# A gated mix of segmented attention and a spectral filter on one core: keys put into order by the copies, wider score and value matmuls, and a new written-out order

## The chip, the cores and the metric

The kernel runs on one core of a Trainium2 chip. The metric is the device time of one execution in microseconds (us). The kernel before was timed in three runs. One more execution was profiled, and every duration here is from that one. Engines are named as the profile names them: PE (TensorE matmul), PEld (TensorE weight load, which overlaps PE), DVE (VectorE), ACT (ScalarE), POOL (GpSimd) and SP (SyncE, which issues most of the transfers).

## The reference

Two branches work on the same 2048 x 640 input, and a gate mixes them row by row. Branch A is attention with 32 heads of 20 over four segments of 512 tokens, each with a linear memory of the segments before it. Branch B multiplies a two-dimensional spectrum with learned weights.

```python
# A: per segment s of 4, 32 heads of 20
logits = einsum('bhqd,bhkd->bhqk', qs, ks) * scale + mask        # causal within 512 tokens
p = softmax(logits);  a_dot = einsum('bhqk,bhkd->bhqd', p, vs)
pq = where(qs > 0, qs + 1, exp(qs))
a_mem = einsum('bhld,bhde->bhle', pq, M) / (einsum('bhld,bhd->bhl', pq, z)[..., None] + 1e-6)
o = g * a_mem + (1 - g) * a_dot                                  # g = sigmoid(beta), per head
pk = phi(ks);  M += einsum('bhld,bhle->bhde', pk, vs);  z += pk.sum(l)
a = concat(o) @ wo
# B
X = rfft2(x) * (w_r + 1j * w_i);  b = irfft2(X).astype(bfloat16)
# mix, per row
g = sigmoid((x * gate_w).sum(-1));  out = g * a + (1 - g) * b
```

## The kernel before, in words

The program is first recorded as a list of operations (`Sched.op`), each with the engines that it may run on, its inputs and outputs and a cost. The tuple `ORDER` then names, for each place in the program, an operation (number // 2) and which of its engines runs it (number % 2). `schedule` does not choose any order: it walks `ORDER`, gives each operation its PSUM bank and its DMA semaphore by a small cost model, and `emit` writes the five in-order engine programs with the waits between them. In that model a matmul costs its columns (`PECOL`), a change of the PE's tile mode costs `COST`, and a transfer costs its time on 16 rings (`ring`). The model of before holds nothing of how an engine's program gets to the engine.

A TensorE operation is recorded by `mms`: a list of matmuls, each of them two instructions in the program, a weight load and a matmul (PE and PEld have 4796 and 4807 rows on the page). All have the line of the helper, L526 (L524 where the helper cuts a 128-wide weight in four). Copies out of PSUM have L535 on ACT and L537 on DVE.

The parts that the change touches:

- **Projection of keys and queries.** `proj_direct` (segment 0, four heads at a time in 32-column tiles) and `proj_tile` (segments 1 to 3, 128 columns). Queries stream all 512 tokens in one matmul. Keys are wanted in the token order 0-127, 256-383, 192-255 and 128-191, 448-511 and 384-447 (`KPOS` and the turned halves), and `token_order` gets it by streaming 2 x 256 tokens, two matmuls for every weight. The copy out of PSUM (`copy_alts`, 512 columns) then keeps the order.
- **Values.** `v_part` makes a block of 128 tokens; for every odd block the halves of 64 tokens are swapped, with four weight tiles of 32 columns for each of the five chunks.
- **Scores.** `qk_unit` does 80 units, each on all four banks of the pool "qk": kind 0 (12 matmuls), kind 1 (16 matmuls, two halves of 64 keys by 320 and 192 queries, four heads each) and kind 2 (24 small ones). The exponential (L1309, on ACT) follows each, the masks on POOL (L1330) follow that.
- **Probabilities times values.** `pv_flipped` (segments 0 to 2) runs `VPIECES`: six pieces by four heads, the last two being the halves of one block of 128 queries.

The start of the program sets much of the order around this. Segment 0's projections (`proj_direct`, names `xT,wq` and `xT,wk` with 32-column tiles) are the first real work of the PE, while the SP queue brings in weights, the input for branch B (`xsb`), tables and filter weights, one transfer after the other and with at most 1.6 MB under way. Segment 1's transposed input (`xT`, a transposing transfer, L558) comes behind them. From then on attention, branch B and the memory are interleaved in all engines until the output projection (L524 and `oTl`), which ends the program.

Of the kernel before, what the change touches and what calls it, by code (L numbers as in the profile page):

```python
# [12 lines left out]
P = 128  # L13
S = 2048
D = 640
H = 32
DH = 20
# [27 lines left out]
class Op:  # L45
    __slots__ = ("id", "alts", "preds", "succs", "prio", "banks", "nbytes", "npred", "eng", "t0", "t1",
                 "stamp", "need_inc", "dyn", "first", "outside", "name", "dma", "key", "xfer", "lock", "mode", "emode", "hold", "width")


class Sched:  # L50
    HOP = 70.0
    TIE = 0.15
    WINDOW = 1600000
# [7 lines left out]
    def op(self, alts, r=(), w=(), prio=0.0, nbytes=0, name="", after=(), dma=False, xfer=0.0, lock=False, mode=0, hold=False, width=16):  # L61
# [6 lines left out]
        o.xfer, o.lock, o.mode, o.hold, o.width = xfer, lock, mode, hold, width  # L68
# [36 lines left out]
        if name in ("gate_tab", "den_gate") and not o.banks:  # L105
# [5 lines left out]
            (0, 3): 105.0, (1, 3): 105.0, (2, 3): 105.0, (3, 0): 105.0, (3, 1): 105.0, (3, 2): 105.0}  # L111

    def schedule(self, pools, order, nsem=56):
# [14 lines left out]
        for i, o in enumerate(pe):  # L128
            o.emode = o.mode
            if o.mode < 0:  # L130
                modes = [held[id(b)] for b in o.banks if id(b) in held]
                if not modes and i and pe[i - 1].emode not in (1, 3):
                    modes = [pe[i - 1].emode]
                for q in pe[i + 1:] if not modes else ():
                    m = q.mode if q.mode >= 0 else held.get(id(q.banks[0]), -1)
                    if m >= 0:
                        modes = [0 if m in (1, 3) else m]
                        break
                o.emode = (modes + [0])[0]
            if o.emode not in (1, 3):  # L140
                for b in o.banks:
                    held[id(b)] = o.emode
# [3 lines left out]
        tied = [False]  # L146
        level = {k: {q: 0.0 for q in v} for k, v in pools.items()}
# [55 lines left out]
        while len(self.order) < len(order):  # L203
# [8 lines left out]
            o = queue[e][pos[e]]  # L212
            if e == "dve" and tied[0] and pos["pool"] < len(queue["pool"]):
                q = queue["pool"][pos["pool"]]
                if all(p.t1 is not None and p.t1 + self.HOP <= t + 30.0 for p in q.preds) and free["pool"] <= t + 1.0:
                    t += self.TIE * q.alts["pool"][1]
# [11 lines left out]
            free[e] = o.t1 = t + occ  # L228
            if e == "dve" and o.lock:
                port = t + occ  # L230
            if o.dma:
                if o.hold:
                    free[e] = max(free[e], max(ring) + 470.0)
# [236 lines left out]
VPIECES = ((0, 0, 512, 0), (1, 512, 384, 128), (2, 896, 192, 320), (2, 1088, 64, 256), (3, 1152, 64, 448), (3, 1216, 64, 384))  # L470
# [3 lines left out]
class Kern:  # L474
# [35 lines left out]
    def mms(self, items, r, w, prio, name="", extra=0.0, mode=0):  # L510
# [17 lines left out]
        op = self.Sc.op({"pe": (f, cost + 22.0 * (name == "qk"), 216.0 if name == "qk" else 141.0)}, r=r, w=w, prio=prio, name=name, mode=mode)  # L528
        return op
# [24 lines left out]
    def dma(self, dst, src, nbytes, r, w, prio, tr=False, name="", after=(), queue="sp"):  # L554
# [9 lines left out]
        if width == 16 and not tr and nbytes >= 200000 and name[:3] == "ld_":  # L564
# [7 lines left out]
        "ld_xn": (450.0, 950.0, 16), "ld_W": (670.0, 450.0, 16), "W_dup": (480.0, 900.0, 16), "ld_beta": (400.0, 120.0, 16), "ld_big": (500.0, 2900.0, 16), "ld_den": (520.0, 150.0, 16),  # L572
# [18 lines left out]
              ((1, 0, 0, 192, 0, 320), (1, 64, 64, 192, 0, 320), (2, 0, 0, 320, 320, 192), (2, 64, 64, 320, 320, 192)),  # L591
# [4 lines left out]
        0, 22, 28, 74, 72, 24, 2, 30, 4, 44, 6, 26, 8, 10, 36, 12, 42, 70, 14, 16, 34, 18, 176, 200, 20, 188, 32, 194, 182, 88, 178, 184, 196, 180,  # L596
        190, 187, 202, 192, 60, 206, 90, 208, 204, 199, 230, 93, 242, 48, 210, 218, 212, 220, 46, 232, 102, 222, 94, 50, 214, 76, 244, 216, 234, 97,
        224, 226, 62, 1070, 236, 78, 314, 238, 229, 81, 246, 1884, 248, 250, 241, 588, 83, 350, 253, 590, 352, 354, 98, 316, 84, 356, 338, 86, 266,
        116, 340, 268, 100, 358, 604, 105, 361, 318, 606, 270, 272, 320, 56, 274, 342, 106, 322, 52, 344, 118, 278, 40, 276, 280, 128, 628, 608, 324,
        54, 282, 130, 290, 630, 38, 346, 108, 292, 133, 326, 294, 328, 330, 110, 296, 112, 284, 349, 332, 632, 986, 298, 286, 300, 334, 135, 289,  # L600
        254, 992, 612, 336, 414, 592, 398, 58, 256, 136, 400, 114, 362, 139, 258, 614, 364, 402, 366, 368, 610, 370, 386, 994, 372, 260, 404, 388,
        622, 64, 390, 416, 980, 596, 140, 302, 624, 418, 1068, 598, 262, 392, 616, 304, 374, 120, 982, 306, 142, 376, 308, 420, 996, 310, 164, 264,
        378, 380, 618, 313, 382, 984, 394, 123, 384, 654, 397, 430, 1072, 600, 1886, 66, 432, 2050, 1888, 620, 988, 406, 434, 2052, 408, 2054, 594,
        2056, 68, 656, 1890, 410, 462, 634, 2058, 464, 1918, 166, 1892, 466, 436, 468, 1894, 412, 2060, 1920, 168, 1922, 124, 1924, 1896, 626, 470,
        1898, 472, 1926, 145, 516, 518, 1928, 520, 1900, 522, 127, 422, 1932, 524, 474, 424, 1902, 526, 1904, 1066, 476, 152, 1906, 478, 426, 480,
        1908, 482, 446, 154, 528, 484, 530, 448, 428, 532, 1910, 534, 157, 486, 438, 536, 450, 646, 1930, 538, 440, 542, 544, 648, 990, 546, 442,
        554, 548, 540, 556, 558, 550, 560, 488, 552, 500, 490, 502, 444, 492, 452, 562, 494, 650, 496, 564, 504, 506, 566, 498, 508, 652, 884, 568,
        2552, 510, 886, 454, 512, 704, 602, 456, 514, 2106, 888, 171, 2108, 458, 640, 158, 2110, 2112, 706, 643, 2114, 636, 2116, 1940, 1914, 1942,
        998, 2080, 460, 1944, 146, 2082, 639, 1912, 2084, 708, 686, 2086, 658, 644, 1952, 688, 2088, 1946, 1916, 2118, 2120, 2122, 2124, 160, 2126,
        1948, 1936, 570, 162, 1954, 1956, 173, 1951, 2128, 1934, 670, 2090, 2130, 878, 672, 1958, 2132, 1960, 880, 1938, 1974, 882, 872, 1963, 680,  # L610
        712, 1976, 660, 1964, 714, 1978, 1980, 1968, 914, 874, 682, 2134, 2136, 877, 2138, 674, 1982, 2140, 2142, 1985, 676, 2092, 1966, 916, 662,
        678, 919, 830, 2094, 664, 148, 832, 2144, 694, 834, 174, 2146, 1992, 2148, 838, 2096, 2098, 1970, 854, 696, 720, 666, 856, 1972, 2100, 2150,
        684, 722, 2152, 2154, 2160, 2172, 690, 2162, 2164, 2174, 1986, 2166, 836, 2168, 2176, 2178, 2170, 668, 1988, 2180, 2102, 2156, 728, 2104,
        2182, 842, 2184, 692, 2158, 730, 2038, 840, 844, 572, 2186, 2040, 846, 962, 1990, 860, 732, 744, 850, 964, 710, 698, 746, 967, 1998, 716,
        2042, 2000, 701, 862, 908, 734, 2044, 2046, 150, 2006, 1994, 2048, 762, 736, 865, 1996, 2008, 764, 920, 2066, 922, 932, 2010, 2189, 925, 718,
        2012, 910, 934, 2002, 738, 2014, 913, 752, 2191, 2004, 937, 724, 2016, 778, 2062, 848, 944, 755, 2018, 780, 748, 946, 2020, 949, 890, 892,
        766, 2022, 2024, 895, 726, 968, 2026, 974, 970, 2029, 976, 750, 972, 786, 740, 956, 979, 2030, 902, 788, 896, 898, 742, 958, 901, 950, 952,
        575, 2032, 790, 802, 961, 904, 782, 926, 955, 804, 756, 796, 907, 852, 866, 798, 759, 938, 868, 577, 928, 800, 940, 871, 760, 942, 770, 579,
        806, 931, 1008, 1010, 2078, 772, 1040, 2554, 2034, 1000, 2556, 1074, 1002, 2036, 2558, 1012, 2074, 1004, 2560, 1015, 2562, 702, 1042, 2064,
        1007, 774, 2288, 2565, 1044, 2586, 784, 2588, 2290, 1047, 1032, 2590, 1034, 2068, 1036, 1016, 2592, 776, 1039, 2070, 2594, 1018, 808, 2596,  # L620
        2280, 792, 1020, 858, 1048, 2282, 2600, 814, 794, 1050, 2076, 580, 768, 582, 1064, 2566, 1052, 2234, 816, 2072, 2284, 2346, 2236, 2568, 2238,
        2292, 2348, 2226, 2240, 1028, 2570, 1031, 2572, 2208, 2192, 2228, 2574, 2195, 2230, 810, 2232, 2576, 2320, 2210, 813, 2522, 2578, 2322, 2608,
        2212, 2524, 2214, 3220, 1116, 1118, 2610, 2526, 1120, 2612, 2528, 2530, 2244, 1123, 2262, 2294, 2580, 2246, 2296, 2264, 2248, 2266, 2614,
        2268, 1054, 2298, 2616, 2250, 2620, 2622, 2582, 2624, 2598, 1056, 2584, 1084, 1086, 1088, 2626, 1059, 2628, 1090, 2300, 2304, 2618, 2642,
        2631, 2324, 2306, 2216, 1076, 1078, 2218, 2632, 2270, 2302, 1080, 2220, 2644, 2272, 1082, 2222, 1142, 2338, 2314, 2602, 2274, 2252, 2276,
        2316, 1022, 2340, 1144, 2646, 2254, 2326, 2648, 2256, 2650, 2318, 2258, 1024, 1146, 1060, 2604, 2332, 2308, 1027, 2652, 2286, 2404, 1062,
        2335, 2654, 1092, 2310, 2406, 1108, 1110, 1148, 1094, 1112, 2312, 2774, 2776, 2778, 2780, 1115, 2656, 2342, 2782, 2328, 1096, 2350, 2828,
# [1028 lines left out]
```

## Time and profile before

| what | value |
|---|---|
| three runs | 254.83, 256.54, 258.51 us; median 256.54 |
| profiled execution | 252.51 us, of which the span from the first to the last instruction is 250.8 us |
| PE busy | 228.6 us (91%), 4796 matmul rows |
| PEld busy | 147.5 us (59%), 4807 rows |
| DVE, ACT, POOL busy | 199.3 us (79%), 197.4 us (79%), 159.8 us (64%) |
| mean granted TensorE clock | 0.992 |
| program transfers (queue q8, kind "instruction") | 38 packets, 0.62 MB |
| all transfers | 53532 packets, 41.00 MB, mean 163 GB/s |

A busy PE in this profile is not a PE at its peak: matmuls overlap, and the end of each is modelled. The profiled execution is 4.0 us below the median of the three runs.

### The profile page before, as it was taken

How to read it: one execution, taken by the hardware profiler on the slowest of the kernel's cores; microseconds unless marked ns; L12 is line 12 of the kernel's file. 1: busy time of each engine (PE TensorE's matmuls, PEld its weight loads, DVE VectorE, ACT ScalarE, POOL GpSimd, SP SyncE). 2: the span in 40 equal slices, each digit the busy share in tenths (PEclk: the TensorE clock that was granted, in tenths of full speed). 3: DMA queues.
4: the chain of work that ended last, by engine and by line, in shares of the span. 5: the costliest groups of instructions: out<-in, count | busy, mean ns of one | idle time of the engine just before them, and what ended most of it. 6: DMA issues, size and time to landing. Idle time of an engine off the chain costs nothing.

```text
span 250.8 us, 11077 instructions
## 1 busy us (share of the span) xinstructions
PE 228.6 (91%) x4796; PEld 147.5 (59%) x4807; DVE 199.3 (79%) x454; ACT 197.4 (79%) x232; POOL 159.8 (64%) x288
## 2 busy tenths in 40 slices
PE   7697699989989899998999997989999999999993
PEld 3465456666654476555656744545554667577782
DVE  1576387887999999979889996888989999983653
ACT  2265377899979999998989987989899998987320
POOL 8535572356977729396569936676479896689510
PEclk9999799999999999999999999999999999999999
DMA  7999902553354873579775778678168698856214
GB/s 224 287 275 296 269 14 64 118 112 77 86 143 137 208 184 101 145 194 205 202 180 169 203 198 233 178 157 226 64 209 205 168 268 119 128 97 132 95 62 107
DMA packets 53532, 41.00 MB, mean 163 GB/s; under 512 B 24684, under 2 KB 51308, under 8 KB 53484
## 3 DMA queue, kind: packets, MB, share of 16 engines
q1 hardware_dynamic: 52300, 39.62, 63.0%
q10 hardware_dynamic: 1184, 0.67, 1.1%
q8 instruction: 38, 0.62, 1.0%
q14 instruction: 10, 0.08, 0.1%
HBM read 21.94 MB, written 11.12 MB: 132 GB/s over the span
## 4 chain that ended last, share of the span: by engine, by line
PE 58%; DVE 17%; DMA 12%; ACT 6%; issue 3%; SPq 2%; POOL 0%; ACTq 0%; DVEq 0%
PE psum L526 53%; PE psum L524 5%; DMA Wt<-Wt 4%; ACT ex L1309 4%; DVE Ac L537 3%; DVE UV L1492 3%; DMA wk<-in_A_wk_dram 3%; DMA out_dram<-ot 3%; DMA gcc<-g_scr 2%; SPq L560 2%; DVE qu L537 1%; DVE ub L537 1%; DVE G L1534 1%; DVE Bt L537 1%; DVE mem L1203 1%
## 5 line engine op out<-in xcount | busy, mean ns | idle before, releaser
L1330 POOL TENSOR_SCALAR_AFFINE_SELECT ex<-ex 128x256 bf16<-128x256 bf16 (+2 forms) x224 | 121.5, 565 | 50.8 <-ACT ex L1309 48.1
L1309 ACT ACTIVATE ex<-psum 128x2048 bf16<-128x2048 f32 (+4 forms) x92 | 138.5, 1505 | 16.3 <-PE psum L526 14.4
L526 PE MATMUL psum<-xT,wk 128*32 128x256 bf16 (+1 forms) x470 | 38.0, 287 | 5.1 <-issue 3.6
L526 PE MATMUL psum<-xT,wq 128*32 128x512 bf16 (+1 forms) x224 | 33.4, 385 | 1.1 <-ACT xT L535 0.8
L526 PE MATMUL psum<-qkp 20*64 20x64 bf16 (+5 forms) x1280 | 32.4, 270 | 0.5 <-ACT ex L1309 0.2
L526 PE MATMUL psum<-wv,xT 128*32 128x320 bf16 (+3 forms) x400 | 31.3, 302 | 0.4 <-DVE va L1161 0.4
L526 PEld LDWEIGHTS psum<-xT,wk 128*32 128x32 bf16 (+1 forms) x470 | 22.6, 101 | 12.9 <-issue 7.3
L1492 DVE TENSOR_TENSOR UV<-psum,Wt 128x642 bf16<-128x642 f32 x32 | 25.0, 817 | 2.8 <-DMA Wt<-Wt 2.2
L526 PEld LDWEIGHTS psum<-qkp 20*64 20x64 bf16 x1280 | 13.3, 103 | 15.5 <-ACT ex L1309 9.1
L524 PE MATMUL psum<-wo,oU 128*32 128x320 bf16 x480 | 20.8, 300 | 0.0
L526 PEld LDWEIGHTS psum<-wv,xT 128*32 128x32 bf16 (+1 forms) x400 | 14.3, 96 | 9.1 <-issue 2.9
L526 PE MATMUL psum<-ex,va 128*32 128x64 bf16 (+3 forms) x576 | 17.4, 256 | 2.0 <-DVE Ac L537 0.8
L1161 DVE TENSOR_TENSOR va<-psum,ebx 128x320 bf16<-128x320 f32 x32 | 14.8, 479 | 5.4 <-PE psum L526 4.4
L526 PE MATMUL psum<-big,Ac 128*128 128x160 bf16 (+2 forms) x96 | 17.6, 258 | 0.8 <-DVE va L1161 0.3
L526 PE MATMUL psum<-big,Cp 128*128 128x321 bf16 (+1 forms) x96 | 17.4, 302 | 0.6 <-DVE G L1534 0.4
L526 PEld LDWEIGHTS psum<-ex,va 128*32 128x32 bf16 x576 | 11.3, 96 | 9.8 <-POOL ex L1330 2.6
L526 PE MATMUL psum<-tt,UV 128*128 128x128 bf16 (+1 forms) x192 | 16.7, 221 | 0.2
L537 DVE CAST ot<-psum 128x320 bf16<-128x320 f32 x19 | 9.2, 490 | 9.0 <-PE psum L524 6.1
L928 POOL TENSOR_TENSOR xsb<-xf 128x320 bf16<-128x320 bf16 (+2 forms) x12 | 9.1, 759 | 11.1 <-DVE xsb L928 6.4
L526 PEld LDWEIGHTS psum<-xT,wq 128*32 128x32 bf16 (+1 forms) x235 | 11.3, 97 | 7.2 <-issue 2.2
L1534 DVE TENSOR_TENSOR G<-eo,psum 128x320 bf16<-128x320 f32 x32 | 14.8, 473 | 0.5 <-PE psum L526 0.2
L524 PEld LDWEIGHTS psum<-wo,oU 128*32 128x32 bf16 x480 | 12.7, 97 | 4.1 <-issue 1.0
(100 smaller groups left out, 391.5 us busy)
## 6 DMA issues: line engine op xcount, KB each, us to landing
qkp<-qk_scr SPq DMA_DIRECT2D x24, 160.0 KB
tt<-tab_tt SPq DMA_DIRECT2D x8, 384.0 KB, 4.4
qk_scr<-qu SPq DMA_DIRECT2D x12, 256.0 KB, 3.7
u_scr<-ub SPq DMA_DIRECT2D x12, 256.0 KB, 4.0
Wt<-Wt SPq DMA_DIRECT2D x8, 321.0 KB, 4.5
xsb<-in_A_x_dram SPq DMA_DIRECT2D x8, 320.0 KB, 4.6
oU<-u_scr SPq DMA_DIRECT2D x15, 128.0 KB, 3.7
out_dram<-ot SPq DMA_DIRECT2D x12, 160.0 KB
```

What stands on the lines that cost most here:

```text
L524: h = e.matmul(dst, wt, r_, start=st, stop=sp_, **{**kw, "tile_position": (0, q), "skip_group_check": True})
L526: h = e.matmul(o_, l_, r_, start=st, stop=sp_, **kw)
L537: alts["dve"] = (lambda e: e.tensor_copy(dst(), src()), 67 + 1.04 * n, 68.0)
L560: return e.dma_start(d_, s_)
L928: self.either(lambda e, dst=dst, src=src, d0=d0, n=n, op=op: e.tensor_tensor(xs.ap(o + dst, [D, 2], [1, n]), xf.ap(src + d0, [321, 2], [1, ...
L1161: self.one("dve", lambda e: e.tensor_tensor(va.ap(i * H * VW + h0 * VW, [VW, nh], [1, DH]), self.ps(bank, 0, [DH, nh], [1, DH]), self.ebx. ...
L1203: fn = lambda e: e.tensor_tensor(self.mem.ap(i * D + 64 * q, [4, 16], [P, 5], [1, 4]), self.ps(bank, 0, [VW, 16], [4, 5], [1, 4]), dn.ap(1 ...
L1309: self.one("act", lambda e, d=d, q=q: e.activation(self.ex.ap(*d), self.ps(bank, *q), ACT.Exp, scale=SC), n, [bank], [self.exb(s, 2 * pr + ...
L1330: self.one("pool", lambda e: e.affine_select(self.ex.ap(e0 + d0, [1280, 4], [1, n], np_=np_), self.ex.ap(e0 + s0, [1280, 4], [1, n], np_=np_),
L1492: self.one("dve", lambda e, rh=rh, UV=UV, Wt=Wt, gp=gp, bank=pb[rh]: e.tensor_tensor(UV.ap(rh * 644, [322, 2], [1, KD]), self.ps(bank, 0, ...
L1534: self.one("dve", lambda e, q=q, n2=n2, bank=bank, eo=eo: e.tensor_tensor(self.G.ap(n2 * D + 639 * q, [1 - 2 * q, 320]), eo.ap(q, [1, 320] ...
```

## The change

A key matmul streams all 512 tokens, as a query matmul does, and the copy out of PSUM puts the tokens into order: it is two instructions of 256 columns now (`key_copy`). An odd value block is two weight tiles of 64 columns instead of four of 32, in a tile mode of its own (4). A score unit of kind 1 takes 128 keys in one matmul instead of twice 64. The last two of `VPIECES` are joined, and the moving operand's pattern swaps the halves. That is 747 fewer matmuls, and with their weight loads 1494 fewer instructions: 320 for keys of segment 0 and 150 for the others, 320 for values, 512 for scores, 192 for probabilities times values.

The cost model now counts the PE program's words (two for a matmul) in blocks of 256; a block can be entered only when its transfer is in, which is asked for when the block before is entered and waits behind the rings. It also lets a transfer issued meanwhile cost more, and gives `ld_beta` a longer time. `ORDER` is replaced as a whole; the numbers of SP's and ACT's own transfers stay the same (219 instructions on SP in both), while their places move.

```diff
+    BLOCK, FIRST, READ, MOVE, TAIL = 256, 196, 900.0, 350.0, 2450.0
...
+            if e == "pe":
+                n = o.words * (4 if o.mode < 0 and o.emode == 2 else 1)
+                if words + n > bound:
+                    t = max(t, fetched)
...
+            if e == "pe":
+                if words + n > bound:
+                    at = max(t + occ * max(0, bound - words) / n - 300.0, 0.0)
+                    moving = at + self.READ + 0.1 * max(0.0, ring[0] - at) + 0.26 * max(0.0, ring[15] - at)
...
+                    fetched = moving + self.TAIL
+                    bound += self.BLOCK
+                words += n
...
-VPIECES = ((0, 0, 512, 0), (1, 512, 384, 128), (2, 896, 192, 320), (2, 1088, 64, 256), (3, 1152, 64, 448), (3, 1216, 64, 384))
+VPIECES = ((0, 0, 512, 0), (1, 512, 384, 128), (2, 896, 192, 320), (2, 1088, 64, 256), (3, 1216, 128, 384))
...
+        op.words = 2 * len(items)
...
-              ((1, 0, 0, 192, 0, 320), (1, 64, 64, 192, 0, 320), (2, 0, 0, 320, 320, 192), (2, 64, 64, 320, 320, 192)),
+              ((1, 0, 0, 192, 0, 320), (2, 0, 0, 320, 320, 192)),
...
-    def token_order(self, which, xT, c):
+    def key_copy(self, which, dst, src, np_, **kw):
 
         if which == "q":
-            return [(0, L, lambda: xT.ap(c * L, [1, L]))]
-        return [(0, 256, lambda: xT.ap(c * L, [256, 2], [1, P])), (256, 256, lambda: xT.ap(c * L + P + 64, [256, 2], [-64, 2], [1, 64]))]
+            return self.Sc.op(self.copy_alts(lambda: dst(0, [1, L]), lambda: src(0, [1, L]), L), **kw)
+
+        def parts():
+            return ((dst(0, [1, 256]), src(0, [256, 2], [1, P])), (dst(256, [P, 2], [64, 2], [1, 64]), src(P + 64, [256, 2], [-64, 2], [1, 64])))
+
+        def act(e):
+            for d, q in parts():
+                h = e.activation(d, q, ACT.Copy)
+            return h
...
+        return self.Sc.op({"act": (act, 2 * 65 + 0.833 * L, 110.0), "dve": (dve, 2 * 67 + 1.04 * L, 68.0)}, **kw)
...
-            items = []
-            for o, n, src in self.token_order(which, xT, c):
-                items.append((lambda c=c, o=o, n=n, src=src: (self.ps(bank, o, [1, n]), w.ap(c * D + t * P, [1, P]), src(), c == 0 and o == 0, c == 4,
-                                                              {"skip_group_check": True}), n))
+            items = [(lambda c=c: (self.ps(bank, 0, [1, L]), w.ap(c * D + t * P, [1, P]), xT.ap(c * L, [1, L]), c == 0, c == 4, {}), L)]
...
-            for p0, t0, n in ((0, 64, 32), (32, 96, 32), (64, 0, 32), (96, 32, 32)) if i % 2 else ((0, 0, P),):
+            for p0, t0, n in ((0, 64, 64), (64, 0, 64)) if i % 2 else ((0, 0, P),):
...
-            self.mms(items, [b("wv"), xb[c], bank] + ([b("gw")] if h0 else []), [], prio, name="vproj", mode=2 * (i % 2))
+            self.mms(items, [b("wv"), xb[c], bank] + ([b("gw")] if h0 else []), [], prio, name="vproj", mode=4 * (i % 2))
...
+                        m = P if kind == 1 else 64
+                        return (self.ps(bank, hh * 512 + o, [1, n], p0=p0, np_=m), pad.ap((4 + gl) * L + KPOS[j] + kc, [1, m], p0=32 * hh, np_=DH),
```

How the two orders deal out the copies, counted in the two engine programs: DVE has 454 instructions before and 477 after, ACT 242 and 236, POOL 292 and 298. Of the key copies, 14 are on DVE (28 instructions of 256 columns) and 9 on ACT (18). DVE also takes six more of the `eo` copies (L535 to L537) and two more of `oTl`; ACT gives these up.

## The prediction, as it was put on record before the run

> **What bounds the kernel now.** I read three views, in this order: the page's slices, the chain that ended last, and the windows and timeline of the places where that chain is not work. The slices first:
>
> ```profile
> PE   7697699989989899998999997989999999999993
> ...
> DVE  1576387887999999979889996888989999983653
> ACT  2265377899979999998989987989899998987320
> ...
> PEclk9999799999999999999999999999999999999999
> ```
>
> From slice 7 on, three engines are near nine tenths at once. Only the first six slices (some 38 us) show PE as low as 6 while DVE and ACT are still lower, and only there does the granted clock fall. The windows put numbers on it: from 40 to 230 us PE is busy 179.59 of 190 us, DVE 167.89 and ACT 171.62. So no engine alone sets the middle, and PE has 10.4 us of waits there. The chain shows the start:
>
> ```profile
> 13.82 6.12 PE psum L526 x175
> 19.95 1.50 issue
> 21.45 4.68 PE psum L526 x120
> 26.13 2.06 issue
> 28.19 7.13 PE psum L526 x134
> 35.32 0.08 issue
> 35.40 17.27 PE psum L526 x279
> ```
>
> From 12 to 52.7 us the chain is PE alone, broken twice by "issue": PE waits for nothing that another engine or a data transfer gives. Both times its program is late. A packet of the queue "instruction" moves at 19.1 and the next at 25.6 us, and PE goes on 2.3 and 2.6 us later. The page counts 38 such packets of 0.62 MB, 16 KB each, which is 256 words of 64 bytes, or 128 matmuls with their weight loads. From the first resumption to the second stall the chain has 120 matmuls, close to one block. After the second stall there is a second loss:
>
> ```profile
> 27.00:28.00 1.00, 0.00 (x0) 0.00 (x0) 0.05 (x1) 0.00 (x0) 0.93 (x3) 1.00 0.98 358
> 28.00:29.00 1.00, 0.81 (x17) 0.67 (x19) 0.00 (x0) 0.00 (x0) 0.77 (x2) 0.53 1.05 334
> 29.00:30.00 1.00, 1.00 (x24) 0.85 (x17) 0.00 (x0) 0.33 (x1) 0.00 (x0) 0.50 1.16 244
> 30.00:31.00 1.00, 1.00 (x21) 0.65 (x12) 0.32 (x1) 0.65 (x2) 0.00 (x0) 0.50 0.95 105
> 31.00:32.00 1.00, 1.00 (x29) 0.40 (x28) 1.00 (x4) 0.15 (x1) 0.44 (x1) 0.76 0.44 92
> ```
>
> The columns are the window, its length, busy time of PE, PEld, DVE, ACT, POOL, the granted clock, DMA share and GB/s. From 28 to 32 us the PE runs at half clock. No one else works for it there either: the transfers are full and DVE and ACT wait for PE.
>
> **The change part by part.**
>
> *Program transfers.* The blocks of 128 matmuls that lie over the stalls hold 3.5 to 4.05 us of column time before, because a 32-column key matmul of 256 tokens takes 27 ns of the PE (8 of them start 0.21 us before the next group) and a query matmul of 512 takes 53. In the new order the keys also take 53, and the same blocks hold 5.97, 6.26 and 9.53 us, counted along both orders with these two durations. A block's transfer took 6.7 us from one entry (21.45) to the next resumption (28.19) under full rings, and about 5 in the stall before. So a block now lasts about as long as its successor needs. I keep 0.3 us of the 3.56 us of stalls. The half clock costs (1-0.53)+(1-0.50)+(1-0.50)+(1-0.76) = 1.7 us, and it goes with the gap. Sum: -3.3 -1.7 = -5.0. Bounds: 0 if the next block is as late again, -5.3 if nothing is left. What hid it: nothing, the chain is on PE throughout. What is late next: the score units' banks and segment 1's input (below).
>
> The Trainium skill ("TensorE: Matmul & The Clock Gate", "HAM oscillation") asks for no idle gaps over some 3.4 us if the clock is to stay. Here a gap of 2.06 us, 4.7 us after one of 1.50, was enough: the measurement decides. By the page's rule alone the clock would not be tied to these gaps, and the 1.7 us would stay.
>
> *Fewer matmuls elsewhere.* They save no column time: a pair of key matmuls of 256 columns holds the PE 0.21 to 0.22 us (36.98 to 37.19, 41.20 to 41.42 for one query matmul of 512). Score units show that the count is not the price either:
>
> ```profile
> 54.85 0.42 PE L526 MATMUL psum<-qkp 20*64 20x320 bf16 x16
> 55.20 0.83 PE L526 MATMUL psum<-xT,wk 128*128 128x256 bf16 x6
> ...
> 57.40 0.43 PE L526 MATMUL psum<-qkp 20*64 20x512 bf16 x12
> 57.76 0.44 PE L526 MATMUL psum<-va,pkn 128*128 128x154 bf16 x4
> ```
>
> 16 matmuls hold the PE 0.35 us and 12 hold it 0.36; both stream 512 columns, 0.21 us, and the other 0.14 us is the way into and out of the small tiles. A kind 1 unit of 8 matmuls is priced like these: 0. Bounds over 32 units: -0.14 each (-4.4) if the overhead were all count, and +0.06 each (+2.0) if its eight 128-column loads go one after the other at 28 ns (24 such loads took 0.67 us at 222.66) instead of 16 in 0.16.
>
> *Copies that put keys in order.* No row has this copy. Nearest rows:
>
> ```profile
> L537 DVE CAST qu<-psum 128x512 bf16<-128x512 f32 x15 | 10.3, 683 | 1.5 <-PE psum L526 1.4
> ...
> L535 ACT ACTIVATE qu<-psum 128x512 bf16<-128x512 f32 x15 | 8.8, 598 | 2.6 <-PE psum L526 2.2 <-DVE phq L1130 0.2
> ...
> L537 DVE CAST Cp<-psum 65x256 bf16<-65x256 f32 x10 | 4.1, 410 | 0.2 <-PE psum L526 0.2
> ...
> L535 ACT ACTIVATE Cp<-psum 65x256 bf16<-65x256 f32 x6 | 2.2, 372 | 0.4 <-PE psum L526 0.4
> ```
>
> By the 256-column rows, which also gather and scatter, two halves are 820 against 683 ns on DVE and 744 against 598 on ACT: 14 x 0.137 + 9 x 0.146 = 1.9 + 1.3 = 3.2 us. Both engines run at nine tenths in the middle and share the copies, so half of the sum reaches the path: +1.6. Bounds: 0 (two halves in a row overlap, as two 320-column copies of ACT took 0.77 us at 234.94 against 0.437 for one), and +4.7 by the 322-column rows (521 and 542 ns): 14 x 0.36 + 9 x 0.49 = 9.4, halved. With the copies that moved from ACT, DVE goes from 199.3 to some 208 us and ACT from 197.4 to some 191.
>
> *Tile modes.* Walking both orders, the PE changes its tile shape 233 times before and 242 after; the 64-column value tiles no longer stand with the 32-column ones. A change is half of the 0.14 us above, 0.07. Nine are 0.6 us; PE waits in the middle anyway, so I charge 0.3 (0 to 0.6).
>
> This speaks against the change, and the Trainium skill says the same ("TensorEngine Tiling (Array Packing)", "Key Properties"): changing the tiling mode drains the PE, while staying within a mode does not. It gives no time, so by it the term could be anything above zero.
>
> *The new order.* Everything in it moved, so I cannot add it up. The amount of PE column time ahead of each score unit is nearly the same in both orders, and so is what is left after the last one. The old order ran 5 us off its own plan from 28 us on, because the stalls were not in it, while DVE, POOL and the transfers went on. Of PE's 10.4 us of waits in the middle I credit a quarter: -2.6. Bounds: -10.4 (all) to +10.4 (as much again).
>
> *Sum:* -5.0 + 0 + 1.6 + 0.3 - 2.6 = -5.7 us. The profiled execution would go from 252.51 to 246.8. The three runs have a median 4.0 us above it, and I take the same difference off that: 256.54 - 5.7 = 250.8 us. About 2% (5.1 us) is what a measurement can tell from no change.
>
> **The rivals.**
>
> 1. *Segment 1's input becomes the wait.* On SP, 5.8 MB now stand ahead of the transposing load of `xT`, 4.24 MB before (seven of the eight `xsb` loads instead of five, and `wv`, come first). 1.56 MB at the 258 GB/s of the first 20 us are 6.0 us, at the 353 to 380 of the best windows 4.2. It was issued at 12.87 and would be at 17 to 19; it lands 8.3 us later, at 25 to 27, if the rings let it. Its first use would move from 35.40 to about 30.4. For it: rings full until 31 us in the rows above, so it may land after 30.4. Against it: 3 to 5 us of slack. If it is 5 us late, the start's gain is gone: 256.54 - 5.7 + 5.0 = 255.8.
> 2. *DVE becomes the bound (slower).* Place: 40 to 230 us, where DVE is the one that ends most of PE's waits and 24 of the 30 half copies of segments 1 to 3 stand on DVE. If half a copy with permuted columns costs what a whole one does, 683 ns, the 14 copies add 9.6 instead of 1.9 us, and DVE's total rises by 8.6 + 7.6 = 16.2, all of it on the path: 256.54 - 5.0 + 16.2 = 267.7. It is slower by 2% from 10.1 us on the path. Against it: the `Cp` rows gather and scatter at no extra cost (680 ns for 512 columns, as for straight copies).
> 3. *The order gains everything:* 256.54 - 5.0 - 10.4 + 1.9 = 243.0. For it: the waits are there. Against it: DVE and ACT at nine tenths leave little room.
>
> That the change does not do what it says (stalls as long as before, in other places) would leave 256.54 + 1.9 - 2.6 = 255.8; it is priced like rival 1 and counted with it.
>
> **How the numbers follow.** Forecast 0.56 (its own range 247 to 255; 0.44 faster by over 2%, 0.12 within), rival 1 with its twin 0.15 (0.13 within, 0.02 slower), rival 2 0.19 (0.18 slower, 0.01 within), rival 3 0.10 (faster). Faster 0.54, same 0.26, slower 0.20. The range runs from 243 (rival 3) to 264, part of the way into rival 2, where the copies cost more than the rows say but not all of it.
>
> **What would show it.** Right: no "issue" piece over 0.5 us in the chain between 12 and 40 us, a granted clock of 1.00 in all windows after 12 us, some 32 instruction packets, the first use of the new `xT` near 30 us, key copies of about 410 (DVE) and 370 ns (ACT), kind 1 score units of 0.35 us. Wrong: a PE wait "DMA xT" near 30 us (rival 1); key copies over 600 ns with PE waiting on DVE longer than before (rival 2); PE idle from 40 to 230 us well over 10 us, which would make the order a loss.

## The result, and the profile after

The changed kernel took 245.72 us (median of four executions, 244.69 to 246.51) beside 255.69 us for the kernel before (four, 252.64 to 258.51). The ratio is 0.968 (95% interval 0.959 to 0.978): faster. Its profiled execution took 245.93 us with a span of 244.1 us and a mean granted clock of 1.000; before, 252.51, 250.8 and 0.992. The sum of the prediction was 246.8 for this execution and 250.8 for the median. Executions of one kernel spread over several us with the granted clock; the ratios, and the medians of set C below, take only executions within 1.5% of the kernel's fastest, and where single executions are compared, their mean clock is given.

The helper of TensorE operations has the lines L547 and L545 now (L526 and L524 before), copies have L557 on ACT and L559 on DVE, and the ordering copies of keys L1005 (ACT) and L1010 (DVE). The slices of the changed kernel, to be set beside those of before:

```profile
PE   7999999979979999999899999998989899799994
...
DVE  0678778979999999988998988999999989784573
...
ACT  2487967979998989989799998988988788686410
...
PEclk9999999999999999999999999999999999999999
```

Slices 2 to 5 of PE were 6, 9, 7 and 6 and are all nines, DVE and ACT are fuller beside them, and no slice of the clock is low. The waits of PE in the first 40 us (us in total, times, longest), the two largest of the kernel before:

```profile
PE psum L526 <- issue: 3.6, 2, 2.1
PE psum L526 <- DMA wk<-in_A_wk_dram: 1.4, 2, 1.3
```

The same view of the changed kernel:

```profile
PE psum L547 <- DVE G L825: 1.3, 1, 1.3
PE psum L547 <- ACT xT L557: 0.2, 1, 0.2
```

The second list is complete (the wait for `G` stood in the first one too). Both stalls of the program are gone, and also a wait for a piece of `wk`, on which the prediction had no word. PE is busy 27.86 of the 28 us from 12 to 40 (24.17 before), and segment 1's `xT` is first used at 27.85 us instead of 35.40:

```profile
27.85 0.59 PE L547 MATMUL psum<-xT,wq 128*128 128x512 bf16 x2
```

The program moves in 32 instruction packets instead of 38.

Copies of the changed kernel, grouped by shape (busy us and mean ns of one, then idle time ahead of them):

```profile
L1010 DVE CAST qu<-psum 128x256 bf16<-128x256 f32 x24 | 8.9, 413 | 0.7 <-PE psum L547 0.7
L559 DVE CAST qu<-psum 128x512 bf16<-128x512 f32 x10 | 6.8, 683 | 0.1
L1005 ACT ACTIVATE qkp<-psum 128x256 bf16<-128x256 f32 x10 | 3.2, 385 | 1.4 <-PE psum L547 1.4
```

A half takes 413 ns on DVE and 385 on ACT, but busy time is less than count times mean, because two halves in a row overlap: 8.9 / 12 = 0.74 us for a pair on DVE (0.683 for the one copy before), 3.2 / 5 = 0.64 on ACT (0.60).

### The profile page after: what moved, and what is told of

Read it like the earlier page. It is cut to its first block, busy times and chain, and to the rows that moved or that the text cites. A ratio compares the mean times of both kernels' runs of the same rounds, so it can differ in the third digit from the quotient of the medians.

```text
span 244.1 us, 9607 instructions
## 1 busy us (share of the span) xinstructions
PE 226.0 (93%) x4037; PEld 134.3 (55%) x4060; DVE 205.4 (84%) x477; ACT 192.8 (79%) x226; POOL 163.5 (67%) x294
## 5 line engine op out<-in xcount | busy, mean ns | idle before, releaser
L547 PE MATMUL psum<-qkp 20*64 20x64 bf16 (+5 forms) x1024 | 31.4, 266 | 1.4 <-ACT ex L1340 0.6
L547 PE MATMUL psum<-wv,xT 128*64 128x321 bf16 (+3 forms) x240 | 30.0, 303 | 1.9 <-ACT qu L1005 1.4
L547 PE MATMUL psum<-xT,wk 128*32 128x512 bf16 (+1 forms) x224 | 30.7, 379 | 1.0 <-DVE UV L1523 0.5
L547 PE MATMUL psum<-xT,wq 128*32 128x512 bf16 (+1 forms) x223 | 30.8, 380 | 0.8 <-ACT xT L557 0.2
L547 PEld LDWEIGHTS psum<-qkp 20*64 20x64 bf16 (+1 forms) x1024 | 12.1, 100 | 18.6 <-ACT ex L1340 9.3
L545 PE MATMUL psum<-wo,oU 128*32 128x320 bf16 x480 | 21.1, 300 | 0.6 <-DVE oU L1614 0.6
L547 PEld LDWEIGHTS psum<-wv,xT 128*64 128x64 bf16 (+1 forms) x240 | 15.4, 105 | 9.9 <-issue 2.0
L547 PE MATMUL psum<-ex,va 128*32 128x512 bf16 (+4 forms) x480 | 17.0, 275 | 1.3 <-POOL ex L1361 0.8
L547 PE MATMUL psum<-big,Cp 128*128 128x321 bf16 (+1 forms) x96 | 17.8, 302 | 0.4
L547 PE MATMUL psum<-big,Ac 128*128 128x321 bf16 (+2 forms) x96 | 16.3, 258 | 1.4 <-DVE Ac L559 0.9
L950 POOL TENSOR_TENSOR xsb<-xf 128x320 bf16<-128x320 bf16 (+2 forms) x14 | 10.5, 764 | 9.5 <-DVE xsb L950 7.7
L547 PE MATMUL psum<-tt,UV 128*128 128x128 bf16 (+1 forms) x192 | 16.4, 221 | 0.1
L547 PEld LDWEIGHTS psum<-xT,wq 128*32 128x32 bf16 (+1 forms) x235 | 10.7, 96 | 10.2 <-DVE Ac L559 0.9
L559 DVE CAST ot<-psum 128x320 bf16<-128x320 f32 x19 | 9.0, 489 | 8.5 <-PE psum L545 4.7
L547 PEld LDWEIGHTS psum<-xT,wk 128*32 128x32 bf16 (+1 forms) x235 | 10.9, 97 | 9.5 <-issue 0.9
L547 PEld LDWEIGHTS psum<-ex,va 128*32 128x32 bf16 x480 | 10.1, 96 | 9.4 <-POOL ex L1361 2.8
L547 PEld LDWEIGHTS psum<-tt,UV 128*128 128x128 bf16 (+1 forms) x192 | 12.4, 102 | 5.2 <-issue 1.6
```

The costliest lines, as they stand in the source:

```text
L545: h = e.matmul(dst, wt, r_, start=st, stop=sp_, **{**kw, "tile_position": (0, q), "skip_group_check": True})
L547: h = e.matmul(o_, l_, r_, start=st, stop=sp_, **kw)
L559: alts["dve"] = (lambda e: e.tensor_copy(dst(), src()), 67 + 1.04 * n, 68.0)
L950: self.either(lambda e, dst=dst, src=src, d0=d0, n=n, op=op: e.tensor_tensor(xs.ap(o + dst, [D, 2], [1, n]), xf.ap(src + d0, [321, 2], [1, ...
```

## The experiments

They were run in three sets, each on one chip beside the kernel before: set A, set B (kernel before: 251.58 to 257.41 us, seven executions) and set C (250.92 to 259.32, 17 executions). In set A six of the seven executions of the kernel before took 255.70 to 261.82 us at mean clocks of 0.974 to 0.986, and one took 250.79 at 1.000. So the distances from it that the expectations of set A name can't be read there; its kernels are compared with one another, and set C repeats three of them beside the changed kernel.

The theory: P, the gain is that segment 0's joined key matmuls no longer outrun the transfers of PE's program at the start; in set C with O, the new order adds some 3 us of its own. The rivals: the number of instructions matters everywhere; the copies cost something that the rest must earn; or the order does it all (what set A calls theory O).

**New matmuls, old order (A).** The changed kernel with the tuple of before:

```diff
     ORDER = (
-        0, 22, 28, 102, 72, 24, ...      (the new order)
+        ...                              (the order of before)
```

> The new matmuls and key copies, played in the order of before. Theory P (the gain is the program's transfers at the start, which depends on how long 128 matmuls last there): no issue piece over 0.5 us on PE between 12 and 40 us, granted clock 1.00 there, segment 1's input first used near 29 us, and 5 to 7 us off the time of before: a ratio of 0.972 to 0.980. Theory O (the gain is the new written-out order): within 1.5 us of before, ratio 0.994 to 1.006, even if the stalls are gone, since the time is given back in the middle.

249.14 us (247.31 to 250.25). No "issue" piece on PE in the first 40 us; first use of `xT` at 30.05 us. The stalls go away without the new order.

**Old matmuls, new order (A).** The reverse.

> The matmuls of before (4807, keys in two pieces, 64-key scores), played in the new order. Theory P: the stalls come back, two or three issue pieces of 1.5 to 2.5 us and a stretch of half clock between 12 and 40 us; 5 to 7 us over the changed kernel, so a ratio to before of 0.99 to 1.00. Theory O: at most 2 us over the changed kernel, ratio 0.970 to 0.977.

254.51 us (253.83 to 255.57). The chain has five "issue" pieces of 0.55 to 1.64 us from 14.75 to 53.38 us, and no window before 40 us is at half clock. The new order alone does not remove the stalls; it spreads them. How they are spaced speaks for the program's blocks:

```profile
15.30 4.00 PE psum L526 x128
19.31 1.64 issue
20.95 4.55 PE psum L526 x128
25.50 0.55 issue
```

Between two stalls stand exactly the 128 matmuls of one block, twice in a row, at the usual pace; the next stall, at 44.98 us, comes 379 matmul rows later, five short of three blocks. The stalls also keep their places in PE's program whatever work stands there: counted in the timelines' matmul rows from the start, they come after 348 and 476 here and in the repeat of this kernel in set C, 349 and 477 in the kernel before (128 between them, where the chain that the prediction read has 120), and 348 in the kernel that follows.

**Only segment 0's keys streamed in two pieces again (A).** The changed kernel with 160 matmuls more:

```diff
-                    return (self.ps(bank, 0, [1, L], ...), w.ap(...), xT.ap(c * L, [1, L]), c == 0, c == 4, ...)
+                for o, n, src in self.token_order(which, xT, c):
+                    ... (self.ps(bank, o, [1, n], ...), w.ap(...), src(), c == 0 and o == 0, c == 4, ...)
-        self.key_copy(which, ...)
+        self.Sc.op(self.copy_alts(...))
```

> The changed kernel with one part undone: segment 0's keys are streamed as twice 256 tokens again, with one straight copy of 512 columns (160 matmuls, 320 instructions more, all in the first 30 us; 8 copies simpler). Theory P: this alone brings back most of the loss, stalls of 3 us or more in all before 40 us, and a time 4 to 6 us over the changed kernel (ratio to before 0.985 to 0.993). Theory O, and the rival that the whole count of instructions matters: at most 1.5 us over it (320 of 1494 instructions, a fifth of the gain).

251.13 us (250.16 to 253.36). Three windows of its profile, with the columns as in the prediction (window, length, PE, PEld, DVE, ACT, POOL, clock, DMA share, GB/s):

```profile
19.00:20.00 1.00, 0.46 (x18) 0.18 (x7) 0.00 (x0) 0.24 (x1) 0.83 (x2) 1.00 1.70 237
20.00:21.00 1.00, 0.00 (x0) 0.00 (x0) 0.00 (x0) 0.00 (x0) 0.00 (x0) 1.00 1.49 65
21.00:22.00 1.00, 0.89 (x35) 0.89 (x38) 0.57 (x1) 0.13 (x1) 0.00 (x0) 1.00 0.51 110
```

The stall is back at the old place: PE stops for 1.65 us until 21.11, with an instruction packet moving in 18 to 19 us. `xT` is first used at 30.41 us, 2.6 later than in the changed kernel. No second stall follows in this order, and the clock stays at 1.00 there: one stall of 1.65 us, where 3 us or more were expected. The time can't be set against the 4 to 6 us expected, since the changed kernel was not in set A and these executions ran at mean clocks of 0.973 to 0.990.

**Only segment 0's keys joined (A).** The kernel before with `proj_direct` and its copy changed as above, in reverse: 320 of the 1494 instructions.

> The kernel before with that one part alone: segment 0's keys in one matmul of 512 tokens and copies that put them into order; everything else, the order too, as before. Theory P: no stall over 0.5 us before 40 us, segment 1's input first used near 29 us, 4 to 6 us faster (ratio 0.977 to 0.985). Theory O and the rival of the whole count: within 1.5 us of before.

249.11 us (247.71 to 249.86), as much as all new matmuls in the old order (249.14), with `xT` first used at 29.55 us. The other 1174 instructions bring nothing that is seen here.

**The changed kernel again, and three parts of it undone (B).** The first is unchanged. In the second a key copy is one straight instruction, so that keys are not put in order. In the third, kind 1 scores go in halves of 64 keys again (512 instructions more). In the fourth, odd value blocks use four 32-column tiles again (320 more).

```diff
-        if which == "q":
+        if True:
```

```diff
-              ((1, 0, 0, 192, 0, 320), (2, 0, 0, 320, 320, 192)),
+              ((1, 0, 0, 192, 0, 320), (1, 64, 64, 192, 0, 320), (2, 0, 0, 320, 320, 192), (2, 64, 64, 320, 320, 192)),
```

```diff
-            ... ((0, 64, 64), (64, 0, 64)) if i % 2 else ((0, 0, P),):
+            ... ((0, 64, 32), (32, 96, 32), (64, 0, 32), (96, 32, 32)) if i % 2 else ((0, 0, P),):
```

> The changed kernel once more, for the three beside it. 244.5 to 246.5 us if nothing of the chip matters; no issue piece over 1 us on PE.

> The changed kernel with every key copy as one straight instruction of 512 columns; left out is the key order of the reference's mask, the work is otherwise the same. Prediction: two halves cost 3.2 us more over DVE and ACT together and half of it is on the path, so 1.6 us faster than the changed kernel beside it (0 to 4.7). Rival: the copies are hidden, within 0.5 us of it.

> The changed kernel with the kind 1 score units in halves of 64 keys again (256 matmuls, 512 instructions more, spread over the whole program). Theory P with the unit's price from the profiles, 0.35 against 0.33 us: 32 x 0.02 = 0.6 us of PE time, so 0 to 1 us slower, unless two more program blocks make a stall. Rival (the gain follows the count of instructions): 512 of 1494, so 2.5 to 3.5 us slower.

> The changed kernel with odd value blocks in four 32-column tiles again (160 matmuls, 320 instructions more, 80 of the matmuls in segment 0). The term for tile modes in the prediction, 0.3 us for all nine changes, says 0 to 0.5 us faster; a program stall near 36 to 42 us, where 44 value matmuls become 88, would make it 1 to 2 us slower; the rival of the count says 1.5 to 2 us slower.

| kernel | median of all four (range), us | executions with mean clock 1.00 |
|---|---|---|
| changed | 248.49 (243.91 to 250.58) | 243.91 |
| one copy | 247.31 (243.65 to 250.35) | 243.65, 244.81 |
| scores by 64 | 247.84 (243.43 to 249.90) | 243.43 |
| values by 32 | 247.27 (244.96 to 251.03) | 244.96, 246.74 |

The changed kernel's median lies above the 244.5 to 246.5 us expected of it. None is slower or faster than it by more than the spread, and the executions at full clock of the first three lie within 1.4 us. So neither the ordering copies nor 512 score instructions have a price that can be told from zero here. With one or two such executions of each this is weak: the kernel before took 252.27 to 254.75 us at mean clock 1.000 in set C, a spread of 2.5 us, so the 1.6 us predicted for the copies would not stand out. The 2.5 to 3.5 us that the count of instructions asks of the scores are unlikely. The values' executions at full clock lie 1.1 and 2.8 us above the changed kernel's only one, which settles nothing. In the first 40 us all three have only the two waits shown above for the changed kernel.

**The square on one chip, and segment 0 alone (C).** Sets A and B do not tell the order's own share, since the changed kernel was not in A.

> The changed kernel once more, as the corner of a square of four (old or new matmuls by old or new order) whose other corners run beside it. Theory P+O (segment 0's joined keys end the program's late transfers at the start, and the new order adds some 3 us on its own): 244 to 248 us, some 3 us under the new matmuls in the old order. Theory P alone (the order's 3 us were the difference of two chips): within 1 us of the new matmuls in the old order.

> New matmuls and copies, order of before. Theory P+O: 248 to 250 us, no issue piece over 0.5 us on PE before 40 us, and 3 us above the changed kernel. Theory P alone: 245 to 247, as the changed kernel.

> Old matmuls and copies, new order. Both theories: issue pieces over 1 us on PE before 55 us again. P+O: 252 to 255 us, so 1 to 3 us under the kernel before, and 6 to 8 above the changed one, since the order only fits when its keys are joined. P alone: equal to the kernel before within 1 us.

> The kernel before with only segment 0's keys joined and put in order by their copies (320 of the 1494 instructions fewer), order of before. Both theories: within 1 us of the new matmuls in the old order, 5 to 7 us under the kernel before; the other 1174 instructions then give nothing. Rival C (the count of instructions matters all over): 3 us or more above the new matmuls in the old order.

| set C | median (range of all), us | ratio to before (95%) | first use of `xT`, us |
|---|---|---|---|
| before | 253.80 (250.92 to 259.32) | | 35.40 (its first profile) |
| old matmuls, new order | 253.11 (251.08 to 256.31) | 1.000 (0.994 to 1.005) | 31.70 |
| new matmuls, old order | 249.84 (247.61 to 251.12) | 0.989 (0.981 to 0.996) | 30.40 |
| segment 0 joined, old order | 247.77 (246.91 to 251.22) | 0.982 (0.974 to 0.990) | 30.70 |
| changed | 246.92 (246.09 to 249.00) | 0.979 (0.972 to 0.986) | 27.49 |

By the medians the matmuls are worth 4.0 us in the old order, the order 0.7 with the old matmuls, and both together 6.9; the ratios give 2.8, 0.1 and 5.2. At 2% the changed kernel's gain, clear in the first measurement, is open in this set (0.980 lies in its interval). Segment 0 alone is worth 6.0 us by the medians and 4.6 by the ratio, at least as much as all the matmuls; it came out 2.1 us below them, where 1 was expected, but the intervals overlap. The new order pays only where its keys are joined, and then 2.9 us (249.84 to 246.92). The intervals of these two ratios still overlap, so this last size is likely and not settled. With the old matmuls the new order has the stalls again. Its timeline on PE, with the idle time before each group in brackets:

```profile
16.01 0.41 PE L526 MATMUL psum<-qkp 20*64 20x64 bf16 x6 [0.45 <-issue]
21.12 1.38 PE L526 MATMUL psum<-xT,wk 128*32 128x256 bf16 x42 [1.10 <-issue]
26.76 0.40 PE L526 MATMUL psum<-xT,wk 128*32 128x256 bf16 x6 [1.10 <-issue]
```

Where the order's share lies, two places in the profiles show. At the start, the old order waits 0.98 us for a piece of `wk` until 12.41 us (the changed kernel 0.2 on this chip), and its first use of `xT` comes 2.9 us later. In the middle, the old order waits for transfers of branch B's filter weights `Wt` and table `tt`. The chain of the kernel with new matmuls and old order, set C:

```profile
136.61 5.24 DMA Wt<-Wt
...
141.87 1.56 DVE UV L1523 x2
...
145.10 4.62 DMA tt<-tab_tt
...
150.38 6.06 PE psum L547 x49
```

The same pair stands in the chain with segment 0 alone joined (`Wt` from 136.37 for 5.42 us, `tt` from 144.94 for 5.62). In the kernel before, two `Wt` transfers stand there (140.90 and 149.48), and PE waits 1.4 us for `tt`. From 130 to 160 us PE is busy 26.71 us in the old order with new matmuls, 26.20 with segment 0 alone joined, 27.61 before, and 29.00 of 30 in the changed kernel of the same set. The group of the filter multiply tells the same, with the idle time of DVE ahead of it; new matmuls in the old order, set C:

```profile
L1523 DVE TENSOR_TENSOR UV<-psum,Wt 128x642 bf16<-128x642 f32 x32 | 25.0, 818 | 3.3 <-DMA Wt<-Wt 2.4
```

The same group in the changed kernel's first profile:

```profile
L1523 DVE TENSOR_TENSOR UV<-psum,Wt 128x642 bf16<-128x642 f32 x32 | 25.2, 820 | 0.9 <-PE psum L547 0.7
```

How much this place is worth can be bounded by the idle time of PE from 130 to 160 us: 2.4 us before, 3.3 and 3.8 in these two profiles of the old order, 3.0 and 2.4 in those of the same two kernels in set A (whose chains have only the `tt` transfer there), and 1.0 in the changed kernel. So the old order may give back up to 1.4 us of the start's gain here, and the new one saves 1.4 to 2.8 us; further on other waits take that back (below). No run moved these transfers alone, so the 2.9 us is not divided exactly between the two places. Nor do the two profiled executions divide it: that of the old order was the slowest of its six (251.12, clock 0.993), that of the changed kernel the fastest (246.09, clock 0.991).

## Why the prediction was right, and what was off

The direction, the class and the range (243 to 264) held. The range held by its width: 245.72 us lies under the forecast's own 247 to 255. By the medians of set C the change is worth 6.9 us, against 5.7 in the sum. Step by step:

- **Program transfers (-5.0).** Right in cause; near in size, but by luck in part. With the old order kept, joining segment 0's keys brings the first use of `xT` forward by 4.7 to 5.9 us in four profiled executions (35.40 to 29.55, 30.05, 30.40 and 30.70); splitting them again brings a stall of 1.65 us back. The 0.3 us kept for late blocks were not needed. The 1.7 us for the half clock belonged to the one profiled execution: three other profiles with stalls (the longest 1.10 to 1.65 us) kept 1.00 before 40 us, and the changed kernel has such a stretch from 193 and from 198 us in its two other profiles. The gain is there without it: at a mean clock of 1.000 set C has 252.27 to 254.75 us for before (five executions) and 247.61 to 249.31 for the new matmuls in the old order (three), 5.3 us apart by their medians. Stalls of 3.56 us would be the larger part of that; where the rest lies no run shows, as the kernel before was profiled once. That the block's column time against its transfer decides was the reading; the runs show that the key matmuls of segment 0 decide it, and didn't vary the block or the transfer by itself.
- **Fewer matmuls elsewhere (0).** Right as far as it was tested. A kind 1 unit holds PE 0.33 us with 8 matmuls (20.03 to 20.36 us in the profile), against 0.35 with 16. In the old order segment 0's 320 instructions alone bring as much as all 1494, and adding 512 back costs nothing that could be seen.
- **Copies (+1.6).** Too high. The durations were right (413 and 385 ns against 410 and 372 predicted), but the step took a pair as twice one. Pairs overlap, and with 0.06 us (DVE) and 0.04 us (ACT) for each the 14 and 9 copies add 14 x 0.06 + 9 x 0.04 = 1.2 us of engine time instead of 3.2. The bound of 0 was the nearer value: copying straight changes nothing that can be measured, though 1.6 us would not have stood out. PE did wait for ACT's ordering copies of `qu`, 1.7 us in the first profile and 0.4 and 0.2 in the two others. DVE's total of 205.4 us and ACT's of 192.8 came out near the predicted 208 and 191.
- **Tile modes (+0.3).** Not settled: the kernel with values in 32 columns is too near the changed one.
- **New order (-2.6).** The size is about right (2.9 by the medians of set C), and that is luck, since the gain lies in other places than said. The step credited a quarter of PE's waits from 40 to 230 us. These waits did not shrink as a whole: PE idles 13.1 us there now, against 10.4 (12.4 and 10.3 in the two other profiles). The prediction had named well over 10 us there as a sign that the order is a loss; the sign came in part, and the order gained all the same. The gain lies at the start, where the step had said that the work ahead of the score units is nearly the same, and in the removed waits for `Wt` and `tt`; other waits came instead, such as 1.7 us for ACT's ordering copies of `qu` and 1.2 for DVE's `mem`.
- **Rival 1** didn't come: the first use of `xT` is not preceded by a wait for its load, though it moved to 27.85 us, earlier than the 30.4 that the rival feared. Its load was issued at 16.3 us and took 5.9, so it was in 5.6 us ahead of its use. **Rival 2** didn't come: DVE is fuller (84% of the span against 79%), but not the bound. **Rival 3**, the order gaining all, would have been 243.0; single executions in set B reach 243.4 to 243.9, the medians don't.
- **From the profiled execution to the median (+4.0).** This is the term that was off most. The sum gave 246.8 for the profiled execution and 245.93 was measured, 0.9 away. But the profiled execution of before happened to lie 4.0 us below its median, and that of after lies 0.2 above its own. Carrying the difference over makes 4.2 of the 5.1 us between the forecast and the median. Over sets A and C, the kernel before took from 250.79 to 261.82 us; a single distance of 4 us inside such a spread is no property of the kernel. Why before spreads so much is only partly known: at a mean clock of 0.998 or more it still took 250.92 to 254.75 in set C.

## What to carry to other kernels

Where PE waits for "issue" in the chain while an instruction packet moves, look at how long the matmuls of a block of its program last: a block that is full of short matmuls can be gone before the next one is in. Joining matmuls was worth it there; no run here shows a gain from it elsewhere merely for the count. After a gain at the start, look at which transfers bound the old order further on, since part of the gain can be lost to them. And put a forecast on the profiled execution; here its distance from a median of three was chance.

## What the runs showed of the hardware

In these profiles the granted clock falls to half after idle time of PE of 1 to 3 us within some 5 us (1.0 us in the second view below; 3.2 and 1.4 us ahead of the two stretches of set C's segment 0 alone joined), but not each time, and not in each execution. Windows of the changed kernel near 192 us, first profile:

```profile
191.00:192.00 1.00, 0.67 (x12) 0.28 (x4) 1.00 (x2) 0.82 (x2) 0.99 (x3) 1.00 1.01 264
192.00:193.00 1.00, 0.37 (x4) 0.22 (x4) 1.00 (x5) 0.37 (x1) 1.00 (x3) 1.00 0.83 252
193.00:194.00 1.00, 1.00 (x29) 0.46 (x32) 1.00 (x5) 0.48 (x2) 1.00 (x3) 1.00 0.60 151
```

The same place in its repeat in set B:

```profile
192.00:193.00 1.00, 0.63 (x4) 0.23 (x3) 1.00 (x2) 0.86 (x2) 1.00 (x3) 1.00 0.48 143
193.00:194.00 1.00, 0.36 (x4) 0.22 (x4) 1.00 (x5) 0.33 (x1) 1.00 (x3) 0.95 0.61 197
194.00:195.00 1.00, 1.00 (x21) 0.33 (x20) 1.00 (x5) 0.44 (x1) 1.00 (x3) 0.50 0.67 178
```

The same work, nearly the same idle time (0.33 + 0.63 and 0.37 + 0.64 us), and only the second execution runs at half clock from then on until about 197.3 us. Leaving aside those in the last microseconds of a program, such a stretch costs 1.7 us each time it is seen (the prediction's sum for the start of before; 0.05 + 3 x 0.50 + 0.16 here), or twice that: 3.4 us from 184 to 191 in the kernel with segment 0 split again. The Trainium skill ("TensorE: Matmul & The Clock Gate", "HAM oscillation") names idle gaps over some 3.4 us; these are all shorter, and the measurement decides. The 1.65 us stall of the split kernel at 20 us left the clock at 1.00. So the clock is one reason why executions of one kernel differ by several us, and why the kernel with fewer stalls isn't free of it.
